# Three chained blocks on one Trainium2 core: the second feed-forward's gate/value projection as seven block products instead of eight, its activations carried through DRAM

## The chip, the cores and the metric

One NeuronCore of one Trainium2 chip runs the whole program. The metric is device time in microseconds (us). TensorE is named PE below and its weight loads PEld; VectorE is DVE, ScalarE is ACT, GpSimd is POOL and SyncE is SP.

## The reference

Everything is float32. Sliding-window attention comes first, then two feed-forward networks (FFNs) over the same 2304 tokens:

```python
x = attention(q, k, v)            # batch 4, 8 heads, 576 positions, head 64; window 128, linear bias
h = x @ w_in                      # (2304, 512) @ (512, 1024)
solu = h * softmax(h)
x = layernorm(solu) * g_ln @ w_out          # back to (2304, 512)
g, val = x @ w_gate, x @ w_val              # each (2304, 512) @ (512, 1536)
return (silu(g) * val) @ w_out2             # (2304, 1536) @ (1536, 512)
```

## The kernel before

Every matrix product of the FFNs is made of three matmul passes over split operands: each operand is a high part (rounded to fp32r by a cast, helper `high`, L213 on ACT or L214 on DVE) and a low part (the rest, helper `low`, L217 on DVE or L219 on POOL); the passes are high*low, low*high and high*high (`HALVES`). Weights come as 64-bit floats and are decoded on the chip by `decode`: a DMA into `dw`, two ACT operations (L236, L240), three DVE operations (L241, L242, L244), one POOL addition (L247, `db<-db,da`), then `high` and `low`.

The order of all instructions on all engines is written out at build time by `Emitter`: generators ask for an engine with an estimated cost and a rank, and a list scheduler picks the next one. Each engine and the one DMA queue (SP) then run their rows in that order, and nothing overtakes. "DVE+" and "POOL+" in the code are never planned at the same time.

The first region holds the attention (`score`, `attend`) and the first FFN: `up(i)` for each of 18 token tiles of 128, its softmax and norm, `flip(i)` (transposes into `lnT`), and `down1(g)` for each pair of tiles. `down1` writes its output, transposed (features on partitions), into `ys` and from there to DRAM (`yscr`).

The second region is the second FFN. `w2` is cut into 12 chunks of 128 hidden features (`c`). A chunk holds gate, value and output weights, 512 columns of decoded floats each. The tokens come in five groups (256 and four times 512). For a chunk and a group, `gate_val` makes gate and value with 12 matmuls each (tiles `gv`; the first two chunks of the first group go into the first region's banks), then Silu on ACT (L799), the product with the value on DVE (L801, `sg`), and the split into `a` (high and low). `down(pas, g)` multiplies the `a` of two chunks by their output weights (tile `o`, 12 matmuls per token tile). A sum over the 12 chunks would not fit in PSUM together with the rest, so each of the six passes adds its `o` to `acc` in SBUF: a copy in pass 0 and L827 on DVE in the five others. Three groups of DMA matter here: `dw<-w`, `ysg<-yscr` and `out<-acc`.

A chunk's first work on `gate_val` waits for its decoded weights and for `y`; in the second region `y` of groups 1 to 4 lies where the first FFN's weights were, so it is loaded after the last `down1`.

Of the kernel before, what the change touches and what calls it, by code (L numbers as in the profile page):

```python
# [18 lines left out]
NT = B * S  # L19
# [3 lines left out]
P = 128  # L23
# [7 lines left out]
CPP = 2  # L31
NPASS = NC2 // CPP
NW2 = 4
NDW = 3
# [8 lines left out]
YS = 2  # L43
# [10 lines left out]
GRP2 = [(0, 256), (256, 512), (768, 512), (1280, 512), (1792, 512)]  # L54
# [25 lines left out]
class Emitter:  # L80
# [84 lines left out]
    def run(self):  # L165
        while self.pending:
            best = {}
            for op in self.pending:
                t, way = min(((max(self.free(w[0]), op[2]), w) for w in op[3]),
                             key=lambda x: x[0] + x[1][1] + BIAS.get(x[1][0].rstrip("+"), 0.0))  # L170
# [3 lines left out]
            t, _, _, op, (engine, cost, fn) = min((x for x in ops if x[0] <= first), key=lambda x: x[1:3])  # L174
# [10 lines left out]
def attention_then_two_ffns(ctx: ExitStack, tc: tile.TileContext, qk, v, w_in, w_out, g_ln, w2, ident_d, base_d, tri_d, out):  # L185
# [6 lines left out]
    yscr = nc.dram_tensor("yscr", [NT // 256, P, KM, 256], F32).ap()  # L192
# [14 lines left out]
    dec = ctx.enter_context(tc.tile_pool(name="dec", bufs=1))  # L207
# [14 lines left out]
    dw_s, da_s, db_s = Slots(NDW), Slots(2), Slots(2)  # L222

    def decode(hi, lo, src, scale=None):
# [3 lines left out]
        yield dw_s  # L228
        words = dec.tile([P, 512, 2], U32, tag="dw", bufs=NDW, name="dw")
# [4 lines left out]
        yield da_s  # L234
        a = dec.tile([P, 512], U32, tag="da", bufs=2, name="da")
        r = yield (ACT, t_act(512), lambda: nc.scalar.activation(a.bitcast(I32), lw, AF.Copy, scale=2.0 ** -29))  # L236
        yield db_s
        b = dec.tile([P, 512], U32, tag="db", bufs=2, name="db")
# [15 lines left out]
        x = yield (low(lo, bf, hi, 512), [x])  # L254
# [395 lines left out]
    def down1(g):  # L650
# [7 lines left out]
        yield ys_s  # L658
        ys = m1.tile([P, KM, 2 * P], F32, tag="ys", bufs=1, name="ys")
        ln = lnT[g]  # L660
        for m in range(KM):
            if m % 2 == 0:
                bk = yield bank_s
                o = banks[bk].rearrange("p (m c) -> p m c", m=2)
            cs = slice(m * P, (m + 1) * P)
            terms = [(wout[c][:, k, cs], ln[a][:, k]) for a, c in HALVES for k in range(KF1)]
            for p in pieces(o[:, m % 2, :], terms, 12, 120.0):
                x = yield p
                yield x
            if m % 2:  # L670
                y = yield (high(ys[:, m - 1:m + 1, :], o, 512, False), [x])
                em.give(bank_s, y, bk)
        em.give(ln_s, x)
        yield x
        down_done[g].settle(x.time)
        x = yield dma(yscr[g], ys, 524288, [y])
        em.give(ys_s, x)
# [3 lines left out]
    wc, yT, acc = {}, {}, {}  # L681
    w2_ok = [[Done() for _ in range(3)] for _ in range(NC2)]
    w2_s = Slots(NW2)
    y_ok = [Done() for _ in GRP2]
    made = {(c, g): Done() for c in range(NC2) for g in range(len(GRP2))}
    aT = {}
    turn2 = [(c, g) for pas in range(NPASS) for g in range(len(GRP2)) for c in range(pas * CPP, (pas + 1) * CPP)]
    granted = [Done() for _ in turn2]
    ysg_s, sg_s, a_s, gv_s, o_s = Slots(YS), {}, {}, Slots(5), Slots(3)
    pools = {}  # L690
    opened2 = Done()
    y_asked = [Done() for _ in GRP2]
    R0 = NTT + LEAD

    def rank2(pas, g, x=0.0):
        return R0 + 1 + pas * len(GRP2) + g + x

    def second_region():
# [4 lines left out]
        pools["w2p"] = ctx.enter_context(tc.tile_pool(name="w2p", bufs=1, side="right", reuse_waits="tile"))  # L703
        sg_s[0], a_s[0] = Slots(1), Slots(CPP)
        new_y(0, pools["w2p"])
        for c in range(NC2):
            em.start(load_w2(c), R0 + PW_2 + 0.1 * c if c < CPP else rank2(c // CPP - 1, 1, 0.2 * (c % CPP)))
        em.start(load_y(0), R0 + PW_2 + 0.05)
        for g in range(1, len(GRP2)):
            em.start(load_y(g), rank2(0, g - 1, -1))  # L710
        for c in range(CPP):
            em.start(gate_val(c, 0), rank2(0, 0, 0.1 * c))
        for g in range(NG1):
            yield stored[g]
        for c in range(CPP):
            yield made[c, 0]
        es1.close()
        pools["m2"] = m2 = ctx.enter_context(tc.tile_pool(name="m2", bufs=1, side="left", reuse_waits="tile"))
        pools["ps2"] = ctx.enter_context(tc.tile_pool(name="ps2", bufs=1, space=PSUM, reuse_waits="tile"))
        sg_s[1], a_s[1] = Slots(2), Slots(CPP)  # L720
        for g in range(1, len(GRP2)):
            new_y(g, m2)
        for tt in range(NTT):
            acc[tt] = m2.tile([P, DM], F32, tag=f"acc{tt}", name=f"acc{tt}")
        opened2.settle(0.0)
        for pas in range(NPASS):
            for g in range(len(GRP2)):
                for c in range(pas * CPP, (pas + 1) * CPP):
                    if (pas, g) != (0, 0):
                        em.start(gate_val(c, g), rank2(pas, g, 0.1 * (c % CPP)))  # L730
# [163 lines left out]
```

## Time and profile before

| what | value |
|---|---|
| median of 3 runs | 844.94 us (843.87 to 846.13) |
| the profiled execution | 845.34 us, its span 843.5 us |
| PE busy | 804.2 us (95%) |
| DVE, ACT, POOL busy | 440.8, 374.8, 236.2 us |
| mean granted clock of PE | 0.985 of 2.4 GHz |

The span runs from the first to the last instruction of the profiled execution; the run's own time is 1.8 us longer. A busy PE is an engine with matmuls in it, which says nothing of their pace; the pace is read from where runs of matmuls start. "x48" in a row means 48 instructions merged.

### The profile page before, as it was taken

Reading aid. Unit: us, or ns where it says so; the run is one execution under the profiler, and the core shown is the slowest. Engines: PE = TensorE matmul, PEld = TensorE weight load, DVE = VectorE, ACT = ScalarE, POOL = GpSimd, SP = SyncE. Lnnn points to the kernel's source line nnn. Section 1 sums busy time; section 2 is a strip of 40 time slices with the busy share of each in tenths; the row PEclk is TensorE's granted clock in tenths of the full one; section 3 lists DMA queues with packets and bytes.
Section 4 is the critical chain, followed back from the end, with each engine's and each line's share of the span. In section 5 each row is a group of like instructions: output and inputs, shape, how many; then the busy total and the mean of one; then the engine's idle time right before and its main releaser. Section 6 shows DMA issues by size and latency. Waiting matters only on the chain.

```text
span 843.5 us, 12981 instructions
## 1 busy us (share of the span) xinstructions
PE 804.2 (95%) x4840; PEld 659.1 (78%) x4840; DVE 440.8 (52%) x1268; ACT 374.8 (44%) x995; POOL 236.2 (28%) x236
## 2 busy tenths in 40 slices
PE   5779799999999999989999999999999999999997
PEld 3556687888788888878788888888888888888885
DVE  4787876465555657755311653364356336533323
ACT  6878975565454655764422531242133115211110
POOL 4566661333222223663000340052025005200000
PEclk9878999999999999999999999999999999999999
DMA  8452213021210005333400220031013002000112
GB/s 287 141 176 70 100 33 125 32 71 42 91 51 26 33 1 202 120 129 105 145 1 1 66 84 1 1 100 51 1 51 99 1 1 76 0 1 26 51 62 88
DMA packets 21983, 57.79 MB, mean 69 GB/s; under 512 B 2592, under 2 KB 3488, under 8 KB 21920
## 3 DMA queue, kind: packets, MB, share of 16 engines
q1 hardware_dynamic: 21920, 56.96, 20.5%
q8 instruction: 38, 0.62, 0.3%
q14 instruction: 25, 0.20, 0.1%
HBM read 47.52 MB, written 9.44 MB: 68 GB/s over the span
## 4 chain that ended last, share of the span: by engine, by line
PE 80%; DVE 7%; ACT 6%; POOL 3%; DMA 2%; issue 1%; SPq 0%; POOLq 0%; ACTq 0%; DVEq 0%
PE gv L555 34%; PE bank L555 18%; PE o L555 18%; PE bank L472 4%; PE bank L371 4%; PE bank L441 2%; POOL db L247 2%; PE bank L637 1%; DVE db L244 1%; DMA ysg<-yscr 1%; ACT e L410 1%; DVE db L241 1%; DVE e L591 1%; DMA dw<-w_in 1%; ACT da L236 1%
## 5 line engine op out<-in xcount | busy, mean ns | idle before, releaser
L555 PE MATMUL gv<-y,w 128*128 128x512 f32 (+1 forms) x1392 | 314.7, 376 | 0.5 <-ACT y L213 0.4
L555 PEld LDWEIGHTS gv<-y,w 128*128 128x128 f32 x1392 | 247.6, 188 | 55.0 <-ACT y L213 0.8
L555 PE MATMUL o<-w,a 128*128 128x512 f32 x648 | 168.0, 394 | 2.4 <-ACT a L213 2.4
L247 POOL TENSOR_TENSOR db<-db,da 128x512 int32<-128x512 int32 x52 | 70.8, 1362 | 298.9 <-DVE db L244 297.5
L555 PEld LDWEIGHTS o<-w,a 128*128 128x128 f32 x648 | 119.9, 188 | 30.9 <-ACT a L213 3.3
L827 DVE TENSOR_TENSOR acc<-acc,o 128x512 f32<-128x512 f32 x90 | 61.8, 687 | 120.9 <-PE o L555 120.9
L555 PE MATMUL bank<-lnT,wout 128*128 128x256 f32 x864 | 116.7, 286 | 4.2 <-ACT lnT L213 4.2
L555 PE MATMUL bank<-win,xs 128*128 128x512 f32 x432 | 117.2, 409 | 1.6 <-ACT bank L597 1.6
L555 PEld LDWEIGHTS bank<-lnT,wout 128*128 128x128 f32 x864 | 108.6, 190 | 9.6 <-ACT lnT L213 4.7
L213 ACT CAST a<-sg 128x512 fp32r<-128x512 f32 (+1 forms) x60 | 34.7, 578 | 171.4 <-DVE sg L801 171.4
L555 PEld LDWEIGHTS bank<-win,xs 128*128 128x128 f32 x432 | 77.8, 192 | 18.9 <-issue 2.8
L801 DVE TENSOR_TENSOR sg<-sg,gv 128x512 f32<-128x512 f32 (+1 forms) x58 | 37.1, 640 | 105.6 <-PE gv L555 92.6
L410 ACT ACTIVATE e<-e,st 128x128 f32<-128x128 f32 (+1 forms) x160 | 63.0, 401 | 21.1 <-DVE st L405 19.0
L799 ACT ACTIVATE sg<-gv 128x512 f32<-128x512 f32 (+1 forms) x58 | 32.4, 559 | 65.8 <-PE gv L555 60.1
L219 POOL TENSOR_TENSOR w<-db,w 128x512 fp32r<-128x512 f32 x36 | 51.0, 1420 | 25.0 <-ACT w L213 24.5
L217 DVE TENSOR_TENSOR a<-sg,a 128x512 fp32r<-128x512 f32 (+1 forms) x60 | 43.2, 719 | 23.3 <-ACT a L213 23.3
L371 PE MATMUL bank<-raw,raw 64*128 64x128 f32 (+2 forms) x576 | 46.3, 303 | 6.6 <-DMA raw<-qk 6.3
L213 ACT CAST w<-db 128x512 fp32r<-128x512 f32 x35 | 21.7, 620 | 64.3 <-POOL db L247 64.2
L371 PEld LDWEIGHTS bank<-raw,raw 64*128 64x128 f32 (+1 forms) x576 | 38.7, 198 | 13.3 <-DMA raw<-qk 6.7
L423 POOL TENSOR_TENSOR e<-e,st 128x256 f32<-128x256 f32 (+1 forms) x58 | 35.1, 612 | 44.0 <-DVE st L416 37.0
L405 DVE CUSTOM_DVE_ANT_0 e<-bank,bias 128x128 f32<-128x128 f32 (+1 forms) x160 | 40.4, 282 | 9.2 <-PE bank L371 4.5
L451 ACT COPY pt<-bank 128x256 f32<-128x256 f32 (+1 forms) x79 | 26.4, 357 | 38.6 <-DVE pt L448 27.3
(64 smaller groups left out, 837.7 us busy)
## 6 DMA issues: line engine op xcount, KB each, us to landing
dw<-w SPq DMA_DIRECT2D x36, 512.0 KB, 3.6
raw<-qk SPq DMA_DIRECT2D x38, 256.0 KB, 3.8
yscr<-ys SPq DMA_DIRECT2D x9, 512.0 KB, 2.9
ysg<-yscr SPq DMA_DIRECT2D x9, 512.0 KB, 3.5
out<-acc SPq DMA_DIRECT2D x18, 256.0 KB, 2.0
dw<-w_in SPq DMA_DIRECT2D x8, 512.0 KB, 4.4
v<-v SPq DMA_DIRECT2D x16, 256.0 KB, 3.4
dw<-w_out SPq DMA_DIRECT2D x8, 512.0 KB, 3.8
```

The lines of the kernel that those rows point to most:

```text
L213: return [(ACT, t_act(n, sbuf), lambda: nc.scalar.copy(hi, src)), (DVEP if sbuf else DVE, t_dve(n, sbuf), lambda: nc.vector.tensor_copy(hi ...
L217: ways = [(DVEP if sbuf else DVE, t_dve(n), lambda: nc.vector.tensor_sub(lo, src, hi.bitcast(F32)))]
L219: ways.append((POOL, t_pool(n), lambda: nc.gpsimd.tensor_sub(lo, src, hi.bitcast(F32))))
L247: x = yield (POOL, t_pool(512), lambda: nc.gpsimd.tensor_tensor(b.bitcast(I32), b.bitcast(I32), a.bitcast(I32), ALU.add), [x, r])
L371: nc.tensor.matmul(banks[ks[r]][0:n, o:o + w], raw[c][0][rows, 2 * qd + j, 0:n], raw[c - 1 + kb][1][rows, 2 * qd + j, 0:w], start=True, st ...
L405: d = yield (DVE, t_dve(P), lambda j=j: nc.vector.tensor_tensor_reduce(e[0:n, j], sc[0:n, j * 256:j * 256 + P], bias[0:n, 2 * pr + j, bs], ...
L410: ex.append((yield (ACT, 93 + t_act(P, True, True), lambda j=j: nc.scalar.activation(e[0:n, j], e[0:n, j], AF.Exp, bias=st[0:n, j:j + 1], ...
L423: eng.tensor_tensor(e[0:n], e[0:n], st[0:n, 6:8].unsqueeze(2).to_broadcast([n, 2, P]), ALU.mult)
L472: nc.tensor.matmul(px[j * 64:(j + 1) * 64, pr, 0:n], src[0:kp, h * 64:(h + 1) * 64], pt[0:kp, late, j, 0:n], start=(late == 1 or t == 0), ...
L555: nc.tensor.matmul(o, terms[m][0], terms[m][1], start=(m == 0), stop=(m == len(terms) - 1))
L801: x = yield (DVE, t_dve(n), lambda: nc.vector.tensor_mul(sg, sg, gv[1][0]), [x, gv[1][1]])
L827: y = yield (DVE, t_dve(512), lambda o=o, tt=tt: nc.vector.tensor_add(acc[tt], acc[tt], o), [x])
```

## The change

The rows of the 512 features are cut into two halves, the columns of gate and value of a chunk are the two column blocks, and the tokens of a group (now 768) are two halves of 384. The 2x2 by 2x2 block product, eight block products before, is made of seven (Strassen's form, in Winograd's arrangement).

- `load_w2(c)` decodes gate and value of a chunk, makes four sums of 256 columns (`add`, L778 on DVE or L779 on POOL) and splits seven blocks into `w2a` tiles of 7 x 256 columns.
- `part_y(p, kk)` loads half of the features of 768 tokens, makes four sums of 384 columns (L828) and splits seven blocks. It runs twice for each of three groups `p`. Group 0 is done during the first FFN's tail, groups 1 and 2 after it.
- `products(s)` runs once for each of 36 pairs of a chunk and a group: seven products of 6 matmuls with 384 columns. Three banks are used for the seven: a product is added in PSUM to what an earlier one left there, after DVE or ACT has read it. The order is 11, s2, s1, 22, s3, s4, a4; s3 waits for the DVE sum `u` (L884), a4 for `v2` (L893). Result: gate and value of both halves, Silu, the product (L904, 768 columns), and one DMA to DRAM (`ascr`).
- The output weights are decoded by `make_wo` and go to DRAM (`wscr`).
- At the end `down(n)` runs for each of 18 token tiles: `load_a` fetches activations of six chunks at a time and splits them, and 36 matmuls of 512 columns add up all chunks in one bank. `acc` is gone.
- No product starts before the last `down1` has ended on PE. `ys` is stored in two halves.

```diff
-GRP2 = [(0, 256), (256, 512), (768, 512), (1280, 512), (1792, 512)]
+    def load_w2(c):
...
+        bg, xg, db_s = yield from unpack(w2[c, :, 0:512])
+        bv, xv, _ = yield from unpack(w2[c, :, 512:1024])
...
+        xa = yield from split(0, bg, 512, [xg])
+        xb = yield from split(2, bv[:, up_], 256, [xv])
+        x1 = yield add(bv[:, up_], bv[:, lo_], bv[:, up_], ALU.add, [xb])
+        x3 = yield add(bv[:, lo_], bg[:, lo_], bv[:, lo_], ALU.subtract, [x1, xg])
+        x2 = yield add(bg[:, lo_], bv[:, up_], bg[:, lo_], ALU.subtract, [xa, x1, x3])
+        x4 = yield add(bg[:, up_], bg[:, up_], bg[:, lo_], ALU.subtract, [xa, x2])
+        xc = yield from split(3, bv, 512, [x1, x3, x2])
+        xd = yield from split(5, bg, 512, [x2, x4])
...
+    def part_y(p, kk):
+        if p:
+            yield opened2
...
+        x = yield dma(r.rearrange("p (a h) t -> p a h t", a=2), src, 786432)
+        sa = yield from split(0, r[:, 0:1], [x])
+        sb = yield from split(1, r[:, 2:4], [x])
+        x3 = yield add(3, 3, 1, ALU.subtract, [x, sb])
+        x1 = yield add(1, 1, 0, ALU.subtract, [x3])
+        x2 = yield add(0, 3, 0, ALU.add, [x3, x1, sa])
+        x4 = yield add(2, 2, 0, ALU.subtract, [x2, sb])
+        sc = yield from split(3, r[:, 0:2], [x1, x2])
+        sd = yield from split(5, r[:, 2:4], [x3, x4])
...
+    def products(s):
+        c, p = order2[s]
+        yield y_ok[p][0]
+        yield w2_ok[c]
+        yield begun2[s - 1] if s else down_done[NG1 - 1]
...
+        x1 = yield product(kx, "11", first=True)
+        x6 = yield product(kd, "s2", first=True)
+        x5 = yield product(kb, "s1", first=True)
+        s1 = yield (ACT, t_act(NH, False), lambda: nc.scalar.copy(t[:, 2], sx), [x1])
+        u = yield (DVE, t_dve(NH), lambda: nc.vector.tensor_add(t[:, 1], sd, t[:, 2]), [x6, s1])
+        s5 = yield (ACT, t_act(NH, False), lambda: nc.scalar.copy(t[:, 3], sb), [x5])
+        f = yield (fair([(DVEP, t_dve(NH), lambda: nc.vector.tensor_add(t[:, 3], t[:, 3], t[:, 2])),
...
+        x2 = yield product(kx, "22", [x1, s1])
+        g1 = yield (ACT, t_act(NH, False), lambda: nc.scalar.activation(t[:, 0], sx, AF.Silu), [x2])
+        x7 = yield product(kd, "s3", [x6, u])
+        v2 = yield (DVE, t_dve(NH), lambda: nc.vector.tensor_add(t[:, 3], t[:, 3], sd), [x7, f])
+        x3 = yield product(kb, "s4", [x5, s5])
+        g2 = yield (DVE, t_dve(NH), lambda: nc.vector.tensor_add(t[:, 1], t[:, 1], sb), [x3, u])
+        x4 = yield product(kd, "a4", [x7, v2])
+        v1 = yield (DVE, t_dve(NH), lambda: nc.vector.tensor_add(t[:, 2], t[:, 2], sd), [x4, f, u])
...
+        x = yield dma(ascr[:, c, p * 2 * NH:(p + 1) * 2 * NH].rearrange("p (h t) -> p h t", h=2), t[:, 0:2], 393216, [x])
...
-            if pas == 0:
-                y = yield (high(acc[tt], o, 512, False), [x])
-            else:
-                y = yield (DVE, t_dve(512), lambda o=o, tt=tt: nc.vector.tensor_add(acc[tt], acc[tt], o), [x])
...
+    def load_a(n, half):
+        x = yield dma(r, ascr[:, cs, tt * P:(tt + 1) * P], 393216)
+        x = yield (high(t[0], r, HB * P), [x])
+        x = yield (fair(low(t[1], r, t[0], HB * P)), [x])
...
+    def down(n):
+                terms = [(t[a][:, c - half * HB], wo[c][:, b], c) for a, b in HALVES for c in (c0, c0 + 1)]
+                        nc.tensor.matmul(o, l, r, start=c0 == 0 and m == 0, stop=c0 == NC2 - 2 and m == 5)
```

Two places in the written order. The first is PE in the middle of the second region. Before, `gv` of a chunk's gate is a row of 12 matmuls over the four feature tiles, and nothing on another engine stands between its passes:

```order
L555 MATMUL gv_4505<-y0_1_4467,w21_3815 128x512 x4
L555 MATMUL gv_4505<-y1_1_4468,w20_3814 128x512 x4
L555 MATMUL gv_4505<-y0_1_4467,w20_3814 128x512 x4
L555 MATMUL gv_4530<-y0_1_4467,w21_3815 128x512 x4
L555 MATMUL gv_4530<-y1_1_4468,w20_3814 128x512 x4
L555 MATMUL gv_4530<-y0_1_4467,w20_3814 128x512 x4
```

Now one `products` set stands in its place; of its 21 rows the first of each product is shown (11, s2, s1, 22, s3, s4, a4), each followed by two more rows of its bank:

```order
L868 MATMUL bank2_79<-yt0_0_3823,w21_4795 128x384 x2
...
L868 MATMUL bank7_84<-yt0_0_3823,w21_4795 128x384 x2
...
L868 MATMUL bank6_83<-yt0_0_3823,w21_4795 128x384 x2
...
L868 MATMUL bank2_79<-yt0_0_3823,w21_4795 128x384 x2
...
L868 MATMUL bank7_84<-yt0_0_3823,w21_4795 128x384 x2
...
L868 MATMUL bank6_83<-yt0_0_3823,w21_4795 128x384 x2
...
L868 MATMUL bank7_84<-yt0_0_3823,w21_4795 128x384 x2
```

The bank of s2 is read by DVE before s3 is added to it and again before a4 is; one product (s4) stands between s3 and a4. This order without gaps holds for most sets; around the second and the thirty-first sets of two neighbours are interleaved.

The second place is DVE just after the last `down1`. Before, the rest of `y` is split there and gate tiles follow:

```order
L214 CAST y0_1_4467<-ysg_3846 128x4x256
L217 TENSOR_TENSOR y1_1_4468<-ysg_3846,y0_1_4467 128x4x256
L217 TENSOR_TENSOR y1_1_4468<-ysg_3826,y0_1_4467 128x4x256
L217 TENSOR_TENSOR y1_2_4470<-ysg_4504,y0_2_4469 128x4x256
L217 TENSOR_TENSOR y1_2_4470<-ysg_4514,y0_2_4469 128x4x256
L801 TENSOR_TENSOR sg_4547<-sg_4547,gv_4530 128x512
```

Now, between the last sum of the first set (L900) and `u` of the second (L884), stand the sums and splits of `y` group 1 (`yt1_1`, raw data in `t6`) and part of chunk 2's decoding (`db_4445`, `w21_4375`):

```order
L900 TENSOR_TENSOR t6_4348<-t6_4348,bank7_84 128x384
L904 TENSOR_TENSOR t6_4348<-t6_4348 128x768
L219 TENSOR_TENSOR yt1_1_4366<-t6_4372,yt0_1_4365 128x384
...
L251 SCALAR_TENSOR_TENSOR db_4445<-dw_4388,db_4445 128x512
L828 TENSOR_TENSOR t6_4372<-t6_4372 128x384
L219 TENSOR_TENSOR yt1_1_4366<-t6_4373,yt0_1_4365 128x384
...
L219 TENSOR_TENSOR yt1_1_4366<-t6_4372,yt0_1_4365 128x2x384
L828 TENSOR_TENSOR t6_4373<-t6_4373 128x384
L884 TENSOR_TENSOR t6_4377<-bank2_79,t6_4377 128x384
```

There are 17 rows between L904 and that L884. On PE the product that waits for this L884 (s3 of the second set) stands after five products of its own set and after the third set's first. In the first region the order is the same up to the last four tiles on PE, and up to the first work of the second region on the other engines.

## Rows read from the trace of the kernel before

**Rows 1.** Page: busy time, and the chain that ended last by engine.
```profile
PE 804.2 (95%) x4840; PEld 659.1 (78%) x4840; DVE 440.8 (52%) x1268; ACT 374.8 (44%) x995; POOL 236.2 (28%) x236
PE 80%; DVE 7%; ACT 6%; POOL 3%; DMA 2%; issue 1%; SPq 0%; POOLq 0%; ACTq 0%; DVEq 0%
```
**Rows 2.** Windows of the second region: PE, PEld, DVE, ACT, POOL busy, clock, DMA.
```profile
406.00:500.00 94.00, 93.23 (x423) 76.04 (x424) 33.93 (x52) 34.56 (x60) 14.80 (x11) 1.00 0.16 51
500.00:844.00 344.00, 338.51 (x1546) 276.55 (x1544) 146.03 (x226) 80.64 (x143) 53.66 (x38) 1.00 0.12 39
```
**Rows 3.** Chain in order of time: start us, us, what.
```profile
472.83 11.20 PE gv L555 x48
```
**Rows 4.** Timeline of PE, first region's end: start, us, operation, idle before and releaser.
```profile
349.73 1.03 PE L637 MATMUL bank<-ident,e 128*128 128x128 f32 x8
353.88 6.02 PE L555 MATMUL bank<-lnT,wout 128*128 128x256 f32 x48 [1.54 <-ACT lnT L213]
361.26 0.98 PE L555 MATMUL bank<-y,w 128*128 128x256 f32 x6 [1.36 <-POOL w L219]
375.87 11.78 PE L555 MATMUL bank<-lnT,wout 128*128 128x256 f32 x96 [2.65 <-ACT lnT L213]
387.48 2.89 PE L555 MATMUL o<-w,a 128*128 128x512 f32 x12
```
**Rows 5.** Groups by form: count, busy us, mean ns, idle before.
```profile
L555 PE MATMUL gv<-y,w 128*128 128x512 f32 x1152 | 283.6, 396 | 0.5 <-ACT y L213 0.4
L555 PEld LDWEIGHTS bank<-lnT,wout 128*128 128x128 f32 x864 | 108.6, 190 | 9.6 <-ACT lnT L213 4.7 <-issue 1.5
L555 PE MATMUL o<-w,a 128*128 128x512 f32 x648 | 168.0, 394 | 2.4 <-ACT a L213 2.4
L555 PE MATMUL gv<-y,w 128*128 128x256 f32 x240 | 32.7, 282 | 0.0
L555 PE MATMUL bank<-y,w 128*128 128x256 f32 x48 | 7.2, 287 | 1.4 <-POOL w L219 1.4
```
**Rows 6.** Timeline, the end of the program.
```profile
839.81 0.69 DVE L827 TENSOR_TENSOR acc<-acc,o 128x512 f32<-128x512 f32 x1 [0.67 <-PE o L555]
```
**Rows 7.** Groups by form, on DVE and POOL.
```profile
L801 DVE TENSOR_TENSOR sg<-sg,gv 128x512 f32<-128x512 f32 x48 | 33.0, 687 | 96.2 <-PE gv L555 92.6 <-ACT sg L799 3.6
L801 DVE TENSOR_TENSOR sg<-sg,gv 128x256 f32<-128x256 f32 x10 | 4.2, 418 | 9.5 <-PE o L555 7.2 <-ACT sg L799 2.2
L241 DVE TENSOR_SCALAR db<-db 128x512 f32<-128x512 f32 x52 | 25.6, 494 | 20.3 <-ACT db L240 20.3
L242 DVE TENSOR_SCALAR db<-db 128x512 uint32<-128x512 uint32 x52 | 30.5, 588 | 0.9
L244 DVE SCALAR_TENSOR_TENSOR db<-dw,db 128x512 uint32<-128x512 uint32 x52 | 39.8, 767 | 0.7
L247 POOL TENSOR_TENSOR db<-db,da 128x512 int32<-128x512 int32 x52 | 70.8, 1362 | 298.9 <-DVE db L244 297.5 <-ACT w L213 1.4
```
**Rows 8.** Timeline of DVE and POOL, 344 to 360 us.
```profile
344.26 1.56 POOL L247 TENSOR_TENSOR db<-db,da 128x512 int32<-128x512 int32 x1
344.71 1.66 DVE L244 SCALAR_TENSOR_TENSOR db<-dw,db 128x512 uint32<-128x512 uint32 x1
348.99 1.28 POOL L247 TENSOR_TENSOR db<-db,da 128x512 int32<-128x512 int32 x1
349.57 0.69 DVE L591 SCALAR_TENSOR_TENSOR e<-bank,e 128x512 f32<-128x512 f32 x1 [0.84 <-ACT e L589]
353.86 1.29 DVE L217 TENSOR_TENSOR lnT<-bank,lnT 128x512 fp32r<-128x512 f32 x2
358.00 1.98 POOL L614 TENSOR_SCALAR e<-e,mst 128x512 f32<-128x512 f32 x2
```
**Rows 9.** DMA issues: KB each, median us from issue to landing.
```profile
ysg<-yscr SPq DMA_DIRECT2D x9, 512.0 KB, 3.5
out<-acc SPq DMA_DIRECT2D x18, 256.0 KB, 2.0
```

More of the change, by code (lines that the diff above doesn't have):

```diff
@@ L42 @@
 VDB = 2
-YS = 2
 PW_2 = -0.5
@@ L690, in attention_then_two_ffns @@
-    pools = {}
[L691 to L696, printed above, removed]
+    wc, yT, wo = {}, {}, {}
+    TAIL = (0, 2, 1)
+    w2_ok = [Done() for _ in range(NC2)]
+    w2_s = Slots(2)
+    y_ok = [[Done() for _ in range(4)] for _ in range(NPR)]
+    YG = [0, 1, 1, 2, 2, 3, 3]
+    made = [[Done() for _ in range(NPR)] for _ in range(NC2)]
+    order2 = [(c, p) for p in range(NPR) for c in range(2)]
@@ L702, in second_region @@
         esa.close()
[L703 to L712, printed above, removed]
+        pools["w0"] = pools["w1"] = ctx.enter_context(tc.tile_pool(name="w2p", bufs=1, side="right", reuse_waits="tile"))
@@ L717, in second_region @@
         es1.close()
[L718 to L730, printed above, removed]
-                em.start(down(pas, g), rank2(pas, g, 1.05 if pas + g else 0.05))
+        pools["w2"] = ctx.enter_context(tc.tile_pool(name="m2", bufs=1, side="left", reuse_waits="tile"))
@@ new lines, in second_region @@
+        for p in (1, 2):
+            pools[f"y{p}"] = (ctx if p == 1 else ey[p]).enter_context(tc.tile_pool(name=f"y{p}", bufs=1, side="left", reuse_waits="tile"))
+            new_y(p)
+        opened2.settle(down_done[NG1 - 1].time)
+        em.give(w2_s, down_done[NG1 - 1])
+        for c in range(2, NC2):
+            em.start(load_w2(c), set_rank(first_use[c], -6.0))
+        for s in range(1, len(order2)):
+            em.start(products(s), set_rank(s))
+        for c in range(NC2):
+            em.start(make_wo(c), set_rank(2 * c + 16))
@@ new lines, in load_w2, with new_y, load_y @@
+        em.give(db_s, xc)
+        xd = yield from split(5, bg, 512, [x2, x4])
+        em.give(db_s, xd)
+        em.give(pair_s, xd)
+        for x in (xa, xb, xc, xd):
+            yield x
+        w2_ok[c].settle(max(x.time for x in (xa, xb, xc, xd)))
+    def new_y(p):
+        yT[p] = [pools[f"y{p}"].tile([P, 7, 2, NH], F32R, name=f"yt{a}_{p}") for a in range(2)]
+    def load_y(p):
+        for g in range(3 * p, 3 * p + 3):
+            yield stored[g]
+        if p:
+            yield fetched[p - 1]
+        if p > 1:
+            yield begun2[2 * p - 3]
+        for kk in range(2):
+            em.start(part_y(p, kk), set_rank(2 * p, -1.2 + 0.1 * kk) if p else R0 + PW_2 + 0.05 + 0.01 * kk)
@@ new lines, in attention_then_two_ffns, with make_wo @@
+    wo_ok = [Done() for _ in range(NC2)]
+    wo_there = [Done() for _ in range(NC2)]
+    aT = {}
+    a_ok = [[Done(), Done()] for _ in range(NTT)]
+    ast_s, a_s, of_s = Slots(2), Slots(4), Slots(2)
+    summed = [Done() for _ in range(NTT)]
+    def make_wo(c):
+        c0, p0 = order2[2 * c + 8]
+        yield made[c0][p0]
+        yield t6_s
+        t = pools["w0"].tile([P, 2, DM], F32R, tag="t6", bufs=2, name="t6")
+        yield from decode(t[:, 0], t[:, 1], w2[c, :, 1024:1536], even=True)
+        x = yield (NONE, 0.0, lambda: None)
+        x = yield dma(wscr[:, c], t.bitcast(F32), 524288, [x])
+        em.give(t6_s, x)
+        yield x
+        wo_there[c].settle(x.time)
```

338 lines of the change are left out of this document (200 added, 138 removed).

## The prediction

> **What bounds the kernel now.** I read the page first: PE is busy 95% of the span, and the chain that ended last is 80% PE [rows 1]. The windows then separate the stages. From 500 us on PE is busy 338.5 of 344 us at full clock, while DVE is busy 146.0, ACT 80.6 and POOL 53.7 [rows 2]. So the second region is PE-bound, with DVE half idle. Since a busy PE says nothing about pace, I take that from starts: 48 matmuls of 512 columns follow each other in 11.20 us, 233.3 ns each [rows 3]; 96 of 256 columns start at 375.87 and the next work at 387.48, 120.9 ns each [rows 4]. The second region is these paces times counts: 1152 x 233.3 + 240 x 120.9 + 648 x 233.3 ns [rows 5] = 449.0 us after 387.48, which gives 836.5; the last matmul's addition begins at 839.81 [rows 6], so only 3.3 us there are waits. From 839.8 to the span's end at 843.5 lie 3.7 us of last addition and store.
>
> **The change, part by part.**
>
> *Products.* Gate and value cost 1152 x 233.3 + 288 x 120.9 ns = 303.6 us now (48 of the 256-column ones lie inside the first region's end). The new form has 36 sets x 7 products x 6 = 1512 matmuls of 384 columns, a width the trace lacks. Scaled from 256 columns one would take 181 ns, scaled from 512 it would take 175; the line through both points gives 177.1, which I take: 267.8 us (264.6 to 274.2). That is 35.8 us less. The Trainium skill (TensorE: Matmul & The Clock Gate, Back-to-back issue gap) gives columns / 2.4 GHz + 2.5 ns, by which 384 columns would be 162.5 ns and the stage 245.7 us; by it 512 columns would be 215.8 ns where the row has 233.3, so I stay with the rows. Weight loads of 190 ns look longer than a 177 ns matmul, but they have the same 190 ns beside matmuls paced at 121 [rows 4, 5], so they don't set the pace.
>
> *Last projection.* 648 matmuls of 512 columns before and after: 151.2 us. What goes is DVE's adding into `acc`, which no matmul waited for: o's waits come to 2.4 us [rows 5]. Now PE needs 36 matmuls, 8.4 us, per token tile, with two fetches of 384 KB. A fetch of 512 KB lands in 3.5 us [rows 9]; ACT and DVE then need about 1 us each for 768 columns, so with two buffers a half tile comes every 3 us or so, where 4.2 are there. The first fetches can start when the 34th set is done, with two sets (14.9 us) of cover. Nothing added.
>
> *First region's end.* All products now wait for the last `down1`. Before, eight rows of six matmuls for the first group filled gaps there (48 x 120.9 ns = 5.8 us), and one stood in front of a `down1` waiting 1.36 us for a weight split [rows 4]. Both go. The chain after: flips near 349.7, a wait of about 1.5 for `lnT` as now, 96 matmuls in 11.6 us, flips 1.9, a wait between 1.5 and the 2.65 that stands there now, 96 in 11.6: the last `down1` ends near 380.5 (378 to 383) instead of 387.5. The last token tile's norm on POOL was done at 360 [rows 8], some 4 us before its flips are due, so it has slack if `y` group 0 and two chunks, now prepared on these engines in place of four chunks, don't hold it up.
>
> *What DVE gets.* A 384-column operation lies between 418 ns (256) and 687 (512) [rows 7]: 0.55 us alone; 768 columns 0.96; two in a row save 0.09 (1.29 for two [rows 8]). A set has five of 384 and one of 768: 3.7 us, 134 us for 36. Chunks 2 to 11 and the output weights are 32 decodings at 494 + 588 + 767 ns [rows 7] = 59 us; splits of 10 chunks 25, of output weights 8; sums on DVE 25 x 0.42 = 10; casts 3; `y` groups 1 and 2 with 16 sums and 15 splits 22. Sum: 262 us alone, about 223 in a row, against PE's 268. DVE goes from half idle to nearly full. ACT gets 2 us per set and stays far below.
>
> *Waits in a set.* s3 waits for `u`, with two products (2.1 us) in between for 0.55 us of DVE: covered. a4 waits for `v2`, which can start only when s3 ends, and s4 (1.06 us) is the only cover for 0.55 us plus the way there and back: about 0.4 us are spare. An operation that DVE began just before (0.60 to 0.96) can eat that. Behind a late `v2` stand that set's other sums and the next decoding; behind a late a4 the whole of PE. Following several sets of the written order with these durations, `v2` comes in time in most, because at this place stand short operations or none. Bounds: 0, and 0.55 (the largest, 0.96, less 0.4) per set, 20 us; nearer to the sets that I followed I take 0.11, 4 us.
>
> *The start of the products.* Here there is no such cover. `y` group 1 may be loaded only after the last `down1`, behind its store on the SP queue; two loads of 768 KB and two of 512 KB for chunk 2 go out in turn. 512 KB land in 3.5 us [rows 9], so the halves are there some 6 and 9.5 us later. Then DVE does what the second order listing shows: after the first set's v1 (8.1 us from the start) the 768-column product and 17 rows, 0.87 + 9.6 us, then `u` 0.47; two decodings' POOL additions of 1.36 us run meanwhile and hold some of it up, by 1.3 us each as a bound. `u` is ready near 20.5. PE has five products of the second set and one of the third until 13.8. So it waits 6 to 7 us for s3. The third set then stands behind more splits (1.5 us), and group 2, split behind the following sets, is late for the fifth by some 3.5. Sum 12 us; lower bound 6 (DVE keeps up in the gaps), upper 16.
>
> *Chunk 11.* In the order its four sums and last two splits come after the thirty-first set's product; by the same durations s2 of the next set waits 2 us (0 to 3).
>
> **Sum**, for a span: 380.5 + 267.8 + 151.2 + 3.7 = 803.2; waits 12 + 4 + 2 = 18; 821.2. The profiled run is 1.8 us longer than its span and 0.4 above the median, so 822.6 on the median's scale, 22 us (2.6%) less than before.
>
> **Rivals.**
>
> *DVE and POOL hold each other up (slower).* The place is every decoding inside the products stage. A DVE operation with both inputs in SBUF took 1.66 us beside POOL's L247, where it takes 0.69 alone; one that reads PSUM took 0.69 beside the same POOL operation [rows 8]. Before, nothing on PE waited closely for DVE. Now f, the splits, the sums and the 768-column product have two SBUF inputs, 32 additions of 1.36 us and 16 shorter ones run on POOL in this stage, and `u` and `v2` are queued behind whatever is held. If each of 32 hold-ups of 0.97 us reaches PE, that is 31 us in place of my 4: 850. It decides from 0.62 us per set above my sum (22.3 / 36). Against it: the written order never plans the two at once, and the operations placed beside POOL's are often those that read PSUM. The Trainium skill (SBUF — State Buffer, Who interferes with whom) says the same as the rows: a DVE instruction with two SBUF inputs contends with GpSimd's reads, and the later one blocks fully. 8%.
>
> *DVE is simply full.* At 262 us alone, with waits for PE between, the stage follows DVE: a tenth of idle time makes it 288 us, 20 beyond PE's 267.8 where I count 18 in all with the 14 of start and chunk 11; that gives 834 to 840. For it: the sum above; against it: operations in a row overlap. 16%.
>
> *The start is hidden.* If DVE does group 1 between other work and `y` lands earlier, the 12 become 3: 813. Steady sets at 0 as well: 809. 14%.
>
> *The round trip through DRAM shows.* If a fetch took 8 us instead of 3.5, half tiles would come every 5 us against 4.2: 36 x 0.8 = 29 us more, 851. The queues were busy only 12% late in the program [rows 2], so 4%.
>
> *The seven products give nothing,* because a 384-column matmul runs at the pace of 512: 1512 x 233.3 = 352.7 us, 85 us more, 907. The two paces in rows 3 and 4 speak against any such step; 1%.
>
> **How the numbers follow.** My forecast, 815 to 833, has 57%; the others stand above. The range 807 to 840 leaves out the slow rivals and part of the fullest DVE, about 17%, and takes in both ends of the starting waits and of the pace. A difference of 0.3% (2.5 us) is about what this kernel's runs tell from no change. Faster by more: 91%; within it 2%; slower 7%, from the first and the last two rivals.
>
> **What would show it.** The last `down1` ending at 378 to 383; 42 matmuls of a set starting over 7.44 us where nothing waits; DVE busy 85 to 95% between there and the last set; s3's wait for L884 of 5 us or more in the second set, waits for L893 under 0.3 us on average; the last 648 matmuls in 151 to 153 us. I am wrong if waits for DVE in the steady sets add up to more than 15 us, if the last projection waits for DMA, or if the first region's end moves past 385.

## The result, and the profile after

The changed kernel takes 830.42 us (median of 4 runs, 829.63 to 832.7) against 844.48 us (843.87 to 846.13) before: a ratio of 0.9835, 95% interval 0.9811 to 0.9859, so 14.1 us (1.7%) less. The forecast was 822.6 us, 22 less; the time is 7.8 us above it and inside the range of the main forecast, 815 to 833. The profiled run took 830.65 us, with a span of 828.9.

First the page (busy time by engine, to set beside [rows 1]) and, of its groups, the two of matmuls that make up the second region:

```profile
PE 776.3 (94%) x4912; PEld 675.2 (81%) x4912; DVE 522.3 (63%) x1439; ACT 420.7 (51%) x1087; POOL 208.4 (25%) x225
...
L868 PE MATMUL bank<-yt,w 128*128 128x384 f32 x1512 | 274.4, 341 | 16.8 <-DVE t L884 6.1 <-DVE t L893 2.6 <-ACT t L885 2.3
L973 PE MATMUL bank<-wo,a 128*128 128x512 f32 x648 | 151.1, 395 | 0.0
```

PE lost 28 us of work and DVE took on 81. The products waited 16.8 us in all, the last projection not at all. Where these waits lie, the timeline of PE shows (start, us, operation, idle before and its releaser; here and below, the first or last row of a listing can be cut off at the edge of the stretch that was asked for):

```profile
354.87 3.36 PE L568 MATMUL bank<-lnT,wout 128*128 128x256 f32 x14 [4.00 <-ACT lnT L215]
...
383.20 11.63 PE L868 MATMUL bank<-yt,w 128*128 128x384 f32 x66
396.72 1.83 PE L868 MATMUL bank<-yt,w 128*128 128x384 f32 x9 [1.89 <-ACT t L885]
399.58 0.79 PE L868 MATMUL bank<-yt,w 128*128 128x384 f32 x3 [1.03 <-DVE yt L219]
405.52 16.71 PE L868 MATMUL bank<-yt,w 128*128 128x384 f32 x84 [5.15 <-DVE t L884]
...
431.73 8.48 PE L868 MATMUL bank<-yt,w 128*128 128x384 f32 x48
...
637.64 33.27 PE L868 MATMUL bank<-yt,w 128*128 128x384 f32 x180 [2.13 <-DVE w L219]
...
674.22 5.99 PE L973 MATMUL bank<-wo,a 128*128 128x512 f32 x25
```

The products run from 383.20 to 674.22, 291.0 us. The longest wait is the second set's s3 for `u`, as forecast; the next is chunk 11's. The windows (PE, PEld, DVE, ACT, POOL busy, clock, DMA) show the clock around the end of three of these waits (the second stretch begins inside its wait; 635.60 to 637.60 is the wait for chunk 11), and the steady sets between:

```profile
354.50:357.50 3.00, 2.63 (x12) 2.63 (x13) 2.84 (x8) 3.00 (x8) 2.00 (x2) 0.56 0.63 244
402.50:408.50 6.00, 2.98 (x9) 2.98 (x10) 5.89 (x10) 4.55 (x8) 0.00 (x0) 0.51 0.00 1
635.60:637.60 2.00, 0.00 (x0) 0.00 (x0) 1.88 (x5) 1.70 (x4) 0.00 (x0) 1.00 0.16 63
638.00:641.00 3.00, 3.00 (x12) 3.00 (x11) 2.05 (x4) 0.28 (x2) 1.28 (x1) 0.52 0.00 0
...
440.00:500.00 60.00, 59.46 (x337) 57.99 (x336) 50.96 (x95) 29.74 (x60) 14.89 (x13) 1.00 0.39 133
500.00:560.00 60.00, 58.66 (x332) 57.06 (x331) 52.71 (x95) 30.91 (x60) 15.37 (x14) 1.00 0.52 176
```

Behind each of these waits PE runs at about half clock (1.2 GHz) for 3 to 4 us; behind the one for `u` the clock had fallen before PE began again. In the steady sets PE is busy 98 to 99% and DVE 85 to 88%.

### The profile page after: what moved, and what is told of

It reads as the page before. It is cut to its first block, busy times and chain, and to the rows that moved or that the text cites. A ratio compares the mean times of both kernels' runs of the same rounds, so it can differ in the third digit from the quotient of the medians.

```text
span 828.9 us, 13683 instructions
## 1 busy us (share of the span) xinstructions
PE 776.3 (94%) x4912; PEld 675.2 (81%) x4912; DVE 522.3 (63%) x1439; ACT 420.7 (51%) x1087; POOL 208.4 (25%) x225
## 4 chain that ended last, share of the span: by engine, by line
PE 61%; DVE 19%; ACT 8%; DMA 4%; issue 4%; POOL 3%; SPq 0%; DVEq 0%; POOLq 0%; ACTq 0%
PE bank L568 20%; PE bank L973 18%; PE bank L868 11%; PE bank L384 4%; PE bank L485 4%; POOL db L254 3%; DVE db L251 2%; DMA dw<-w 2%; PE bank L454 2%; ACT da L243 1%; DVE w L219 1%; DVE db L248 1%; PE bank L650 1%; DMA dw<-w_in 1%; ACT db L247 1%
## 5 line engine op out<-in xcount | busy, mean ns | idle before, releaser
L868 PE MATMUL bank<-yt,w 128*128 128x384 f32 x1512 | 274.4, 341 | 16.8 <-DVE t L884 6.1
L868 PEld LDWEIGHTS bank<-yt,w 128*128 128x128 f32 x1512 | 264.6, 190 | 26.3 <-DVE t L893 8.5
L973 PE MATMUL bank<-wo,a 128*128 128x512 f32 x648 | 151.1, 395 | 0.0
L973 PEld LDWEIGHTS bank<-wo,a 128*128 128x128 f32 x648 | 121.5, 188 | 29.3
L254 POOL TENSOR_TENSOR db<-db,da 128x512 int32<-128x512 int32 x52 | 71.0, 1366 | 238.6 <-DVE db L251 233.3
L219 DVE TENSOR_TENSOR a<-ast,a 128x768 fp32r<-128x768 f32 x36 | 34.5, 958 | 103.6 <-ACT a L215 103.6
L215 ACT CAST a<-ast 128x768 fp32r<-128x768 f32 x36 | 30.1, 836 | 61.2 <-DMA ast<-ascr 61.1
L592 DVE TENSOR_REDUCE mst<-bank 128x1 f32<-128x512 f32 x36 | 24.7, 688 | 31.4 <-PE bank L568 31.3
L243 ACT ACTIVATE da<-dw 128x512 int32<-128x512 uint32 x52 | 34.9, 672 | 18.3 <-POOL db L254 10.4
L897 ACT ACTIVATE t<-t 128x384 f32<-128x384 f32 x36 | 18.9, 525 | 49.5 <-DVE t L895 49.4
L904 DVE TENSOR_TENSOR t<-t 128x768 f32<-128x768 f32 x36 | 39.7, 1104 | 2.2
L454 PE MATMUL bank<-ident,e 128*128 128x128 f32 (+1 forms) x160 | 32.0, 298 | 8.3 <-ACT e L434 5.4
```

The source lines that it names most:

```text
L219: ways = [(DVEP if sbuf else DVE, t_dve(n), lambda: nc.vector.tensor_sub(lo, src, hi.bitcast(F32)))]
L454: nc.tensor.transpose(tp[:, j, 0:n], e[0:n, j], ident[0:n, 0:n])
L868: nc.tensor.matmul(o, l, r, start=first and m == 0, stop=m == 5, skip_group_check=True)
L904: x = yield (fair([(DVEP, t_dve(2 * NH), lambda: nc.vector.tensor_mul(t[:, 0:2], t[:, 0:2], t[:, 2:4])), (POOL, t_pool(2 * NH), lambda: nc ...
L973: nc.tensor.matmul(o, l, r, start=c0 == 0 and m == 0, stop=c0 == NC2 - 2 and m == 5)
```

## The experiments

### An eighth product

```
+        x1 = yield product(kx, "11", [x1])
```

> The changed kernel with an eighth product in every set: the product 11 is made twice into its bank, which adds 36 x 6 = 216 matmuls of 384 columns and no work for another engine (product 11 then counts twice in the output, the one part that differs). Theory A, TensorE sets the pace of the products and the other engines have room: 216 x 177.2 ns = 38.3 us more, less the steady waits that the longer set swallows (3.7 us after 440 us and the 2.1 us before chunk 11, at most), so 830.4 + 33 to 38 = 863 to 869 us. Theory B, VectorE is the bound at 84 to 88% busy and seven products buy only part of their time: a set with eight products would run close to the pace of seven, so under 850 us.

862.59 us (859.98 to 863.03), 32.2 more than the changed kernel. PE's work grew by 36 us, its waits fell by 6:

```profile
L868 PE MATMUL bank<-yt,w 128*128 128x384 f32 x1728 | 310.7, 339 | 11.0 <-DVE t L894 5.0 <-DVE t L885 4.3 <-ACT t L886 0.4
```

The eighth product is paid for, nearly in full: the time comes from matmuls left out. 32.2 lies just under A's 33. (Here, as in every run below but the one with filled waits, the planner made a new order for all engines, so a difference of a few us can hold some of that order's own.) With eight products in this form the kernel is 2.0% slower than before.

### More work for VectorE

```
+        for _ in range(2):
+            v1 = yield (DVEP, 0.0, lambda: nc.vector.tensor_tensor(t[:, 2], t[:, 2], t[:, 2], ALU.max), [v1])
```

> The changed kernel with two more VectorE operations of 128x384 in every set (the maximum of a tile with itself, which leaves the values as they are), behind the last addition of the set, off the chain that TensorE waits for. That is 72 x 0.55 us, or 72 x 0.47 us where they follow each other, = 34 to 40 us of VectorE work, and VectorE is idle for about 12 to 16% of 7.5 us = 0.9 to 1.2 us in a set, nearly the same 0.94 to 1.1 us. Theory A, TensorE sets the pace: 0 to 8 us more, from waits for VectorE's sums where its queue backs up. Theory B, VectorE is the bound: the whole 34 us or more, about 865 us.

870.08 us (865.7 to 872.58), 39.7 more: B's number. Not all of it is VectorE's. Waits in the products rose by 14.4 us, the matmuls themselves took 9 more, and 11.6 us are a wait for `wo` from DRAM in the last projection, while DVE's busy share in the steady sets stayed at 86 to 89%. But part of it is: from 440 to 620 us PE waits 11.0 us for VectorE's sums `u` and `v2` (first two rows: us in total, times, longest), in the changed kernel 2.9 (last two):

```profile
PE bank L868 <- DVE t L884: 8.0, 14, 1.6
PE bank L868 <- DVE t L893: 3.0, 6, 0.8
...
PE bank L868 <- DVE t L893: 2.0, 7, 0.5
PE bank L868 <- DVE t L884: 0.9, 2, 0.7
```

The planner had been told that the two operations cost nothing; so the cost given to it was put right:

> The run with two more VectorE operations in each set, with their cost (468 ns each) given to the planner, which in that run had been told 0; so the engines' orders are planned with them. That run took 870.1 us, 39.7 more than the changed kernel, of which 11.6 us were a wait for weights from DRAM, 14.4 us longer waits for VectorE's sums, and most of the rest slower matmuls. Theory A, VectorE has the room (0.9 to 1.2 us idle a set against 0.94) and an order made without knowing of them was to blame: 835 us or less with it. Theory B, VectorE has no room left in truth: still 855 us or more. Between the two, both count.

865.76 us (862.93 to 870.02): that order was to blame for 4.3 us at most. The waits for the two sums from 440 to 620 us are 8.3 us, that for `wo` 12.1. Then one operation instead of two, planned:

> The changed kernel with one more VectorE operation of 128x384 in every set (36 x 0.47 to 0.55 us = 17 to 20 us of VectorE work), its cost known to the planner. Two of them cost 35 us when planned. Theory A, TensorE sets the pace and VectorE has a margin that the second operation used up: the first costs 0 to 6 us, the time is under 837. Theory B, VectorE and TensorE are in balance already, so that VectorE's work shows in the time one for one: 845 to 850 us.

851.05 us (850.34 to 852.03), 20.6 more for 17 to 20 us of VectorE work: B again, even a little above. Where it goes is the surprise. From 440 to 600 us PE waits 2.1 us, as in the changed kernel; but after 600 us the waits come to 18.9 us, in the changed kernel to 3.8, and one of them takes 11.36 us. PE's rows, and what SyncE, ScalarE, VectorE and GpSimd did before the long wait's end:

```profile
604.61 2.40 PE L868 MATMUL bank<-yt,w 128*128 128x384 f32 x12 [0.65 <-DVE t L893]
610.03 5.50 PE L868 MATMUL bank<-yt,w 128*128 128x384 f32 x30 [3.01 <-DVE w L219]
617.18 26.82 PE L868 MATMUL bank<-yt,w 128*128 128x384 f32 x150 [1.66 <-DVE t L893]
655.36 31.33 PE L868 MATMUL bank<-yt,w 128*128 128x384 f32 x168 [11.36 <-ACT t L883]
688.94 6.33 PE L868 MATMUL bank<-yt,w 128*128 128x384 f32 x24 [2.26 <-ACT t L883]
...
643.58 0.33 SPq L207 DMA_DIRECT2D dw<-w  x1
...
647.29 0.66 ACT L243 ACTIVATE da<-dw 128x512 int32<-128x512 uint32 x1 [4.29 <-DMA dw<-w]
651.58 0.41 ACT L215 CAST w<-db 128x256 fp32r<-128x256 f32 x1 [3.08 <-POOL db L254]
...
642.82 0.69 DVE L251 SCALAR_TENSOR_TENSOR db<-dw,db 128x512 uint32<-128x512 uint32 x1
648.53 0.43 DVE L248 TENSOR_SCALAR db<-db 128x512 f32<-128x512 f32 x1 [1.06 <-ACT db L247]
652.01 0.42 DVE L219 TENSOR_TENSOR w<-db,w 128x256 fp32r<-128x256 f32 x1 [1.87 <-ACT w L215]
...
650.28 1.26 POOL L254 TENSOR_TENSOR db<-db,da 128x512 int32<-128x512 int32 x1 [5.36 <-DVE db L251]
```

This is the last weight chunk. Its second half was fetched only at 643.58, right behind the end (643.51) of the first half's L251, which frees a buffer of fetched words; and DVE, ACT and POOL, each with idle time, hand it to one another while the set's copy (L883) stands in ACT's queue behind its casts. By the code a decoding needs buffers that earlier ones hold: two for the fetched words (until DVE's L251), a single one for the low words (`da`, held from L243 to POOL's L254), two for the result. In the changed kernel ACT's L243 waited 10.4 us in all for `da`:

```profile
L243 ACT ACTIVATE da<-dw 128x512 int32<-128x512 uint32 x52 | 34.9, 672 | 18.3 <-POOL db L254 10.4 <-DMA dw<-w_in 4.2 <-DMA dw<-w 3.7
```

### The same work with the buffers free

This run tells the two readings apart: VectorE has the work of the run with one more operation (536.3 us busy, there 540.1). The buffer of the fetched words now holds the low ones too, until GpSimd's addition.

```
-DEC2 = (2, 1, 2)
+DEC2 = (2, 1, 3)
...
+        else:
+            a = lw
...
-        em.give(d["da"], x)
+        em.give(d["da" if d["n"] is not DEC2 else "dw"], x)
```

> The run with one more VectorE operation in each set (851.05 us, 20.6 more than the changed kernel), and the decodings no longer share one buffer for the low words: ScalarE writes them back over the fetched words, and the 2 KB that this frees are a third buffer for decoded words. VectorE's work is the same as in that run. There the largest loss was one wait of 11.4 us before the first set of chunk 11, whose last fetch was issued at 643.6 us only, while VectorE, GpSimd and ScalarE stood idle in turn for one another. Theory A, the price of the extra operation is one of the decodings' queue: each hands its buffers on later, the delays add up along the 36 decodings, and chunk 11 is late; with the buffers free the wait goes and the time is 831 to 839 us. Theory B, VectorE and TensorE are in balance and VectorE's work itself is paid for: 847 us or more.

826.52 us (824.08 to 827.02): 24.5 us less than the run with the same VectorE work, and 3.9 less than the changed kernel with 36 operations fewer. Its windows, and PE's timeline over the place of the 11.36 us wait:

```profile
440.00:500.00 60.00, 59.76 (x338) 58.29 (x337) 54.17 (x102) 32.03 (x64) 13.45 (x12) 1.00 0.39 132
500.00:560.00 60.00, 59.81 (x334) 57.47 (x334) 56.23 (x106) 33.94 (x66) 17.54 (x15) 1.00 0.52 176
...
599.80 65.37 PE L872 MATMUL bank<-yt,w 128*128 128x384 f32 x365
```

DVE is 94% busy in a stretch in which PE waits 0.2 us of 60, and at least 365 matmuls run without a listed wait through the change to chunk 11. So VectorE had room for this operation; what had none was the decodings' queue, and its delays came out late in the stage. That they add up along all 36 decodings is a reading, not a measurement. Which of the two, the low words' place or the third result buffer, gives how much of it was not separated, nor what the new order gives by itself; and two more operations with the buffers free were not run.

### Less work for VectorE and GpSimd

```
-        x = yield (DVEP, t_dve(512, True), lambda: nc.vector.tensor_scalar_max(bf, bf, MIN_HIGH), [x])
+        if d["n"] is not DEC2:
+            x = yield (DVEP, t_dve(512, True), lambda: nc.vector.tensor_scalar_max(bf, bf, MIN_HIGH), [x])
```

> The changed kernel with one VectorE operation less in each of the second part's 36 decodings: the floor put under the smallest weights is left out (none of this case's weights is that small). That is 36 x 0.43 = 15.5 us less VectorE work. Theory A, TensorE sets the pace: only what of the 16 us of waits in the products is due to VectorE's load can go, 2 to 6 us, so 824 to 828. Theory B, the balance holds on this side too: nearly the whole 15 us, so 816 or less.

824.29 us (821.68 to 825.78), 6.1 less, as A has it: of 15.5 us of work less only 40% show. Waits in the products are 12.2 us (16.8), and from 612.64 on 294 matmuls follow each other, so the wait for chunk 11 is gone here too. The operation left out is also a step of every decoding, so this run doesn't tell VectorE's load from the decodings' queue.

> The changed kernel without GpSimd's additions of the low word in the second part's 36 decodings (the weights lose their low bits, the part left out; the order on the engines is planned anew). They are 36 x 1.37 us of GpSimd time, and the VectorE operation beside one takes 0.7 to 1.1 us longer than its like. Theory A, VectorE's and GpSimd's hold-ups sit mostly in VectorE's own slack: the waits in the products fall by a part of 16 us, and the time by 2 to 6 us, to 824 to 828. Theory B, the hold-ups are what the waits are made of: they go nearly whole and with them the half-clock stretches, 10 us or more, to 820 or less.

827.37 us (824.96 to 827.62): 3.0 less, in A's range, though the two kernels' intervals (0.9775 to 0.9812 and 0.9811 to 0.9859 of before) just touch. The whole of GpSimd's additions, with all that they hold up on VectorE and in the decodings, is worth about 3 us, net of what the new order did: the products begin 2.0 us earlier, and the wait for `u` in the second set grew from 5.15 to 7.36 us.

### The order at the start

The `y` groups' rank -1.2 becomes -0.9:

> The changed kernel with the preparation of the activations' groups 1 and 2 ranked behind the second and the fourth set's additions: in VectorE's queue the first sum u of set 1 stands ahead of the group-1 splits and sums, not behind them. Theory A, the 5.1 us wait of TensorE at 399.6 to 405.5 is one of order alone: it goes, and the time falls by 4 to 6 us, to about 825. Theory B, it is one of the amount of work: VectorE has to finish group 1 before set 2 can start whatever the order, so the wait moves from set 1's sum to set 2's first use of group 1, and the time stays within 1.5 us of 830.4.

842.16 us (836.73 to 844.75), 11.7 more, which neither theory had. At the start B is right as to the place: `u` is in time, but PE then waits for `v2` and for the third set's `y`, and in the last projection for `wo`:

```profile
401.09 4.18 PE L868 MATMUL bank<-yt,w 128*128 128x384 f32 x12 [3.06 <-DVE t L893]
407.46 0.69 PE L868 MATMUL bank<-yt,w 128*128 128x384 f32 x1 [2.19 <-ACT yt L215]
415.29 24.99 PE L868 MATMUL bank<-yt,w 128*128 128x384 f32 x126 [7.14 <-ACT yt L215]
...
672.63 7.15 PE L973 MATMUL bank<-wo,a 128*128 128x512 f32 x30
687.57 0.80 PE L973 MATMUL bank<-wo,a 128*128 128x512 f32 x1 [7.79 <-DMA wo<-wscr]
```

Chunk 2's rank offset -6.0 becomes -4.0:

> The changed kernel with the decoding of weight chunk 2 ranked behind the preparation of the activations' group 1 (chunk 2 is not used before set 6, about 428 us). Between 385 and 405 us that decoding holds VectorE for 7 operations, 3.8 us, and its two GpSimd additions lie beside two VectorE operations that took 1.1 and 0.7 us longer than their like. Theory B, the start is bound by the amount of VectorE work ahead of group 1: the waits before 410 us fall by 3 to 5 us, and the time with them, to 825 to 828 us. Theory A, only the place of set 1's sum u in the queue matters: it still stands behind group 1, the wait shrinks by what went from ahead of it as well, but then u alone shows it and the run with u first gains more than this one. A third, the start is bound by the landing of group 1 (5.2 us) and not by VectorE: no change.

837.0 us (836.12 to 839.23), 6.6 more, with the products done 6.0 us earlier:

```profile
668.19 7.15 PE L973 MATMUL bank<-wo,a 128*128 128x512 f32 x30
683.66 0.79 PE L973 MATMUL bank<-wo,a 128*128 128x512 f32 x1 [8.32 <-DMA wo<-wscr]
685.73 14.55 PE L973 MATMUL bank<-wo,a 128*128 128x512 f32 x55 [1.28 <-DMA wo<-wscr]
```

B holds in the products: the start is bound by how much stands ahead of group 1. But what was put off pushed the last two output-weight decodings behind the products, and their way through DRAM showed: 9.6 us of waits, 2.3 of matmuls at half clock. The same with `make_wo` ranked `2 * c + 10`:

> The run with chunk 2 late, and besides the twelve decodings of the last projection's weights (make_wo) ranked 6 places of a set earlier, 2c + 10 in place of 2c + 16. With chunk 2 late the products ended at 668.2 us, 6.0 us before the changed kernel's 674.2, but then TensorE waited 9.6 us for the last two weight chunks on their way back from DRAM, and those matmuls ran at half clock for a while. Theory A, this wait is the only thing that turned the 6 us won into 6.5 us lost, and it is one of order: the wait goes, and the time is 830.4 - 6 = 824 to 826 us. Theory B, VectorE has no room for the decodings earlier either: what goes at the end comes back as waits for sums in the products, and the time is 830 us or more.

843.6 us (841.77 to 845.14): the wait for `wo` is gone, and an 11.5 us wait before chunk 11's first set stands in its place, behind the same L883 in ACT's queue as above. B's number, and B as far as the loss comes back in the products. That the decodings' queue had no room, more than VectorE, is likely from the run with free buffers; this order was not run with them.

### PE kept busy in the waits

26 overwritten matmuls in front of the second set's s3; 14 and 10 likewise in front of the `down1` at 354.87 and of chunk 11's set:

```
+            def fill(f3=q[2]):
+                for m in range(26):
+                    nc.tensor.matmul(banks[kz][:, 0:NH], w[0][:, 0, 0:P], y[0][:, 0, 0], start=(m == 0), stop=(m == 25))
+                f3()
```

> The changed kernel, every engine's order as it is, with matmuls whose results are overwritten put in front of three matmuls that wait: 14 of 512 columns (3.3 us) into the 4.0 us wait for lnT at 350.9, 26 of 384 columns (4.6 us) into the 5.15 us wait at 400.4, 10 of 384 columns (1.8 us) into the 2.1 us wait for chunk 11 at 635.5. They end before the waited-for value is there, so they delay nothing. Theory A, the half-clock stretches behind these waits (354.4 to 357.9, 402.2 to 409.0, 637.7 to 641.1 us at 1.2 GHz) cost 1.5 + 1.8 + 1.5 us: with TensorE kept busy the granted clock stays 1.00 in all three and the time falls by 3 to 5 us, to 825.5 to 827.5. Theory B, the slow matmuls behind a wait only use time that VectorE's next sum takes anyway: the clock stays up and the time is within 1 us of 830.4.

828.75 us (827.85 to 829.42), 1.7 less: between the two. The clock is 1.00 in all three places; the first product starts at 381.55 in place of 383.20, and the last projection at 672.20 in place of 674.22:

```profile
352.00:357.00 5.00, 4.20 (x27) 3.51 (x26) 4.84 (x14) 5.00 (x13) 2.99 (x3) 1.00 0.82 264
402.00:408.00 6.00, 4.19 (x22) 3.71 (x22) 5.90 (x11) 3.05 (x6) 0.00 (x0) 1.00 0.01 1
636.00:641.00 5.00, 4.45 (x25) 4.14 (x25) 3.04 (x7) 2.26 (x6) 1.30 (x1) 1.00 0.00 0
...
412.98 7.55 PE L873 MATMUL bank<-yt,w 128*128 128x384 f32 x42 [0.81 <-DVE t L916]
642.74 26.36 PE L873 MATMUL bank<-yt,w 128*128 128x384 f32 x150 [0.66 <-DVE t L916]
```

So A holds at the first place, where 1.65 us come through (0.3 of them lie ahead of the fill: the flips before it begin at 348.66, in the changed kernel at 348.96). B holds in the products: 0.4 us for both fills, since faster matmuls only reach the next late sum sooner (last two rows: waits for `v2` that the changed kernel doesn't have there). The gain at the first place and that of the missing floor together:

> The run without the floor, with the 14 matmuls of 512 columns in the wait for lnT besides (their results are overwritten). In the run with all three waits filled the products began 1.65 us earlier from this one, while the other two fills gave 0.3 us together, since VectorE's next sum was no earlier. If what the clock costs before the products comes through to the end: 1.5 to 2 us below the run without the floor. If VectorE's work at the start takes it back: the same time.

821.85 us (820.31 to 823.32), a ratio of 0.9734 (0.9712 to 0.9756) to before: 2.4 below the run without the floor, a little more than the fill's 1.65, and the fastest run here. The free buffers together with these two, without the added operation, were not run.

## Why the prediction was right, and where it was off

**Direction and cause: right.** The gain is that of 216 matmuls left out, as the eighth product shows; the layout around them costs what the forecast gave it, and 7.7 us more of the span: 2.7 before the products and 5.2 in them, less 0.2 behind.

**Pace: right on average, partly by luck.** From 430.41 on, 267 matmuls take 47.31 us, 177.2 ns each against 177.1 from the line between 256 and 512 columns. But this row holds short breaks. Where there are none, 48 matmuls take 8.48 us (from 431.73), the last of them 0.34: that is 173.2 ns from start to start, 2% under the line. The line's 3.9 ns too many, 5.9 us over 1512 matmuls, stood in for breaks that the sum left out. The Trainium skill's 162.5 (TensorE: Matmul & The Clock Gate, Back-to-back issue gap, where the formula is that of an isolated matmul) is not borne out by either figure.

**First region's end: 2.7 us too early.** 383.2 for 380.5, just outside the stated 378 to 383. The mis-sized term is the first wait for `lnT`: 4.0 where I took "about 1.5 as now", with half clock behind it. Of the 2.7 us, 1.3 to 1.65 are the clock, by the fills; the rest I can only read off the timeline: casts and sums of `y` group 0 and chunk decodings stand between the flips' splits on ACT and DVE. The prediction named this work, for the norm on POOL ahead of the flips only, and then left it at nothing.

**Products: 291.0 us for 285.8** (267.8 of matmuls and 18 of waits). The waits were right in sum, 16.8 for 18, and in place: 10.4 up to 440 us where I had 12, v2 2.6 for 4, chunk 11 2.1 for 2. In the parts there was luck: `u` was ready 22.3 us after the products' start where I had 20.5, and s3's wait of 5.15 for my 6 to 7 is short only because PE had lost 1.89 and 1.03 us before it, in waits that I had not named. What the sum left out is PE's own time: 274.4 us busy for 267.8, and 12.5 more than 1512 times the undisturbed 173.2 ns. Each of 20 waits breaks the row, and by the profile, which models where a matmul ends, a last matmul takes 0.34 us in place of 0.17: an estimate of 3.3 us. Some 3 are the half clock, by the windows (two stretches in which 3 to 4 us of matmuls take twice their time). The rest, about 6, lies in slow first matmuls and in breaks too short to be listed; I have not taken it apart. With the clock kept up the busy time fell to 272.4, but the stage only to 290.7 us. So the half clock was hardly a loss of its own there; had I added it to the waits, I would have counted it twice.

**Chunk 11: right number, incomplete reason.** I derived 2 us from the order of VectorE's sums and splits. In the trace that is so: VectorE is busy for 1.88 of the 2.0 us up to the wait's end. But when that work can begin is decided by the decodings' buffers, as the two runs with one more operation show: with the shared buffer the wait grew to 11.4 us, without it there is none, with the same VectorE work.

**Last projection and end: right.** 151.1 us for 151.2 without a wait, 3.5 for 3.7.

**The rivals.** *DVE and POOL hold each other up*: 31 us as priced, about 3 by the run without the additions, its new order included. The hold-ups are there (the 768-column product took 1104 ns on average, 0.95 us alone), but they mostly fall into time that VectorE has. *DVE is simply full*: refuted for the changed kernel's steady sets, since with the buffers free 94% busy costs PE 0.2 us of 60. Yet one operation more cost 20.6 us through the decodings' queue, so the kernel stood nearer to that time than I knew, for another reason; with two more, 35 to 40 us, late sums of VectorE are part of it, and how much is left of it with the buffers free stays open. *The start is hidden*: no; moving `u` forward moved the wait to `y`. *The round trip through DRAM*: I priced the activations' fetches, which never showed, and not the output weights' way through `wscr`. In the changed kernel the last `wo` fetch goes out at 673.42 and takes 6.6 us (the median), and its chunk is needed after 30 matmuls, at 681.2: an estimate of 1.2 us to spare. In four runs, those of two added operations and of the two later preparations, this margin was gone, and the wait was 9.2 to 12.1 us. *Seven products give nothing*: refuted.

## What to carry to other kernels

Price a new matmul width on the line between two paces that the trace shows (2% too high here), add something for every break in the row, and check that the work around it has room in its queue and not just on its engine: a busy share of 85% said little here, while the few buffers that a chain of three engines hands on set the price of one added operation. Delays of background work show at its tail; look at the last chunk and at the last load. When you put work off, ask which deadline it meets next: three reorderings that looked harmless ended 6.6 to 13.2 us above the changed kernel, each with waits of 9 us or more at the far end.

## What the runs showed of the hardware

The clock's fall doesn't follow from the length of a wait alone. In the changed kernel 150 matmuls in a row and a wait of 2.13 us were followed by a clock of 0.52 (near the level of 1.2 GHz) at 638 to 641 us. In the planned run with one more VectorE operation a wait of 3.01 us before 610.03 left it at 1.00 (2.4 GHz), through the wait and after it (12 matmuls had run between that wait and one of 0.65 us before, as its rows above show):

```profile
607.00:610.00 3.00, 0.02 (x1) 0.00 (x0) 3.00 (x6) 1.64 (x3) 0.15 (x1) 1.00 0.00 0
610.00:613.00 3.00, 2.97 (x17) 2.98 (x18) 1.94 (x4) 0.02 (x1) 1.28 (x1) 1.00 0.97 310
```

So what a wait costs in clock must be read row by row. In the run with free buffers GpSimd's integer addition reads its second input at every other word of the fetched tile (`dw`) in 36 decodings, and from a packed tile (`da`) in 16; its duration in ns, least, median and most:

```profile
L258 POOL TENSOR_TENSOR db<-db,dw x36: 1298/1322/4597, 335.3 to 646.7; 128x512 int32<-128x512 int32 x36
L258 POOL TENSOR_TENSOR db<-db,da x16: 1259/1293/1614, 8.0 to 108.4; 128x512 int32<-128x512 int32 x16
```

By the medians reading every other word costs 2%. The mean of the 36 is 1532 ns (1324 for the 16), but a few long ones make it: the longest took 4.6 us.
